# Output stores cut into 32-row pieces, a deeper put-aside window and a reordered prologue in a fused attention and two-layer MoE kernel

## The chip, the cores and the metric

The kernel runs on one core of a Trainium2 chip. The metric is the time of one execution on the device, in microseconds (us). The engines are PE (TensorE, matrix multiply; PEld is its weight load), DVE (VectorE), ACT (ScalarE), POOL (GpSimd) and SP (SyncE, which here issues transfers only). Transfers are issued from the queues of SP and ACT.

## The reference, cut to what matters

Three stages follow one another. For 8 batches of 8 heads, 576 positions and 64 columns, a softmax of `phi` over the positions condenses k and v to 32 memory rows per head, and q attends to those. The result, a matrix x of 4608 tokens by 512, goes through a gated layer (512 to 1536 and back) and then through a squared-ReLU layer (512 to 2048 and back). All is float32.

```
a = softmax(phi over s);  k_m = a^T k;  v_m = a^T v
attn = softmax(q k_m^T / 8) v_m               # -> x, 4608 x 512
xn = x / rms(x) * rms_g
x = (silu(xn @ w_gate) * (xn @ w_val)) @ w_out
out = relu(x @ w_in2)**2 @ w_out2             # 4608 x 512, written to out
```

## The kernel before, in words

Float32 products are made from float32r matmuls: each operand is split into a high and a low part (`split`: ACT rounds, line 67; the low part is a subtraction on DVE or POOL, line 71), and three matmuls stand for one.

The **prologue** computes the attention of batch 0 and prepares the first weights. The weights arrive as 64-bit values and are converted: `conv_next` starts one conversion (two ACT instructions, lines 101 and 102) and ends the one started before (two DVE instructions, lines 110 and 111, and one on POOL, line 115). The attention steps are p1 to p7 (softmax of `phi`), a2 to a7 (memory rows, transposed q), a8 and a9 (scores, lines 388 and 403), a10 to a15 (their softmax, up to the transposed `an`), a18 to a20 (output x, its squares by ACT, and their sum over the columns, line 482), a21 to a23 (reciprocal root of the mean square, from line 493, and scaling). `warm` issues idle matmuls. Instructions of an engine run in the order in which the code names them.

**Phase A** runs 8 batches in 24 slots each: matmuls for g and v (from line 803), Silu on ACT (line 849), and y, one slot later. The steps of the next batch's attention and the conversions of the remaining weights are spread over positions "a" to "d" of the slots by a plan written out by hand (`make_plan`, `slot`). y goes to memory (y1).

**Phase B** takes tokens in five pairs of column groups, the first four wide (512 columns for each half of a pair). In a pair, eight steps q make h from x by seven products in place of eight (a Strassen scheme: `h_S`, `h_A`), square it, and feed one half of the pair's columns straight into z (four PSUM banks, one for each 128 tokens); the other half of g is put aside in memory (`gd`), since the banks hold only one half. Then comes zz: a loop over f = 0 to 15 loads the put-aside tiles back (`gb`, issued on ACT's queue by `gb_load`, so many tiles ahead), splits them (`gbh`, `gbl`) and multiplies them, 12 matmuls for each f. Beside this loop the x tiles of the next pair are loaded (`x2_load`, tile `xr`) and split (`x2_step`), and the next weights are loaded (`wi2_load`: two `si` tiles and, from the second pair on, `wihb` and `wilb`).

Results leave through `out_store` (and `out_last` for the last four tiles): a PSUM bank of 128 tokens by 512 is copied to a tile `os`, and stored. The tokens lie such that 128 rows of a tile are 4 positions j of 32 rows p each, while in the output row number p * 18 + j of a batch is meant; so the destination of one store is an access pattern of 4 by 32 rows of 2 KB. A tile that crosses a batch's end takes two stores.

Of the kernel before, what the change touches and what calls it, by code (L numbers as in the profile page):

```python
# [9 lines left out]
F32 = mybir.dt.float32  # L10
# [10 lines left out]
P = 128  # L21
# [31 lines left out]
class Kernel:  # L53
# [548 lines left out]
    def make_plan(self):  # L602
        self.early, self.warm_ps = 0, None
        self.w1, self.wo, self.wph, self.wpl, self.anh, self.anl = {}, {}, {}, {}, {}, {}


        groups = [(0, hf, fs) for fs in (range(NF1 // 2), range(NF1 // 2, NF1)) for hf in range(2)]
        groups += [(b, hf, range(NF1)) for b in range(1, B) for hf in range(2)]
        self.items = [(b, hf, f, f == fs[0], f == fs[-1]) for b, hf, fs in groups for f in fs]

        def gv(ch):
            return [(kind, ch, cp) for kind in "gv" for cp in range(2)]

        def o(*fs):
            return [("o", f, 0) for f in fs]

        keys = gv(0) + gv(1) + o(0, 1) + gv(2) + o(2, 3, 4, 5) + gv(3) + gv(4) + o(6, 7) + gv(5) + o(8, 9, 10, 11)
        keys += [(c, f, 0) for f in range(NF2) for c in "iz"]
        self.raw_keys, self.conv_keys = keys, list(keys)

        self.plan = {}

        def at(n, pos, step, b, *args):
            if b < B:
                self.plan.setdefault((n, pos), []).append((step, (b, *args)))


        steps = [
            (1, "a", 0, "a7", 0),
            (1, "a", 0, "load_q", 2),  # L630
            (1, "d", 0, "t1"),
            (1, "d", 0, "a3", 0),
            (2, "a", 0, "a7", 1),
            (2, "a", 0, "load_q", 3),
            (2, "b", 0, "a2"),
            (2, "c", 0, "a3", 1),
            (2, "d", 0, "a4"),
            (0, "d", 1, "load_phi"),
            (3, "b", 0, "a5"),
            (3, "c", 0, "a6"),  # L640
            (3, "c", 0, "a7", 2),
            (3, "d", 1, "load_kv", 0),
            (4, "c", 0, "a7", 3),
            (4, "d", 1, "load_kv", 1),
            (5, "b", 0, "a8", 0),
            (5, "c", 0, "a9", 0),
            (5, "d", 1, "load_q", 0),
            (6, "b", 0, "a8", 1),
            (6, "c", 0, "a9", 1),
            (6, "d", 1, "load_q", 1),  # L650
            (7, "c", 1, "p1"),
            (8, "c", 0, "a10", 0),
            (9, "b", 1, "p3"),
            (9, "c", 0, "a10", 1),
            (11, "b", 1, "p4"),
            (11, "c", 1, "p5"),
            (12, "a", 0, "a12", 0),
            (12, "a", 0, "a12", 1),
            (12, "a", 1, "p6"),
            (13, "b", 0, "a13", 0),  # L660
            (13, "d", 0, "a13", 1),
            (14, "c", 0, "a15", 0),
            (15, "a", 0, "a15", 1),
            (15, "b", 0, "a18", 0, 0),
            (15, "c", 0, "a19", 0, 0),
            (15, "d", 0, "a18", 0, 1),
            (15, "d", 0, "a19", 0, 1),
            (16, "c", 0, "sq_add", 0),
            (16, "c", 1, "p7"),
            (17, "b", 0, "a18", 1, 0),  # L670
            (17, "c", 0, "a19", 1, 0),
            (17, "d", 0, "a18", 1, 1),
            (17, "d", 0, "a19", 1, 1),
            (18, "c", 0, "sq_add", 1),
            (19, "b", 0, "a20", 0),
            (19, "c", 0, "a21", 0, 0),
            (20, "c", 0, "a21", 0, 1),
            (21, "a", 0, "a23", 0),
            (21, "b", 0, "a20", 1),
            (21, "b", 0, "an_split", 0),  # L680
            (21, "c", 0, "a21", 1, 0),
            (22, "c", 0, "a21", 1, 1),
            (23, "c", 0, "a23", 1),
            (24, "d", 0, "an_split", 1),
        ]
        for ch in range(NCH):
            i = 14 + 2 * ch
            steps += [(i - 3, "d", 0, "wst_load", ch), (i, "a", 0, "wp_mm", ch), (i, "b", 0, "wp_ev", ch)]

        at(1, "c", "a21", 0, 1)  # L690
        at(2, "a", "a23", 0, 1)
        at(2, "d", "an_split", 0, 1)
        for b in range(B - 1):
            for i, pos, ahead, step, *args in steps:
                if (b, step) == (0, "t1"):
                    step = "t1_first"
                at(NI * b + i, pos, step, b + 1 + ahead, *args)

        for n, ch in ((1, 1), (3, 2), (7, 3), (10, 4), (13, 5)):
            at(n, "c", "wp_mm", 0, ch)  # L700
            at(n, "c", "wp_hi", 0, ch)
            at(n, "d", "wp_lo", 0, ch)
# [19 lines left out]
    def prologue(self):  # L722
# [31 lines left out]
        self.a6(0)  # L754
        self.a7(0, 2)
        self.a7(0, 3)
        self.conv_next()
        self.conv_next()
        for hf in range(2):
            self.a8(0, hf)  # L760
            self.a9(0, hf)
        self.warm(16)
        self.conv_next()
        for r in range(NR):
            self.a10(0, r, "dve")
            self.a12(0, r)
        self.conv_next()
        self.a13(0, 0, "dve")
        self.a15(0, 0)
        self.a13(0, 1, "dve")  # L770
        self.a15(0, 1)
        self.conv_next()
        self.p1(1)
        self.warm(16)
        for hf in range(2):
            for cp in range(2):
                self.a18(0, hf, cp)
                self.a19(0, hf, cp)
            if hf == 0:
                self.p3(1)  # L780
                self.p4(1)
                self.p5(1)
                self.p6(1)
        self.a20_first(0, 0)
        self.a21(0, 0, 0)
        self.wp_mm(0, 0)
        self.wp_hi(0, 0)
        self.wp_lo(0, 0)
        self.a21(0, 0, 1)
        self.a23(0, 0)  # L790
        self.an_split(0, 0, "dve")
        self.a20_first(0, 1)
        self.early = None


# [228 lines left out]
    def phase_b(self):  # L1024
# [32 lines left out]
        def gb_load(end):  # L1057
            while len(loaded) < min(end, NF2):
                i = len(loaded)
                loaded[i] = work("gb", 4, f"gb{p}_{i}", w)  # L1060
                nc.scalar.dma_start(loaded[i], gd[i])

        for _ in range(2):
# [1 line left out]
        for p in range(NPAIR):  # L1065
# [3 lines left out]
            for q in range(NQ):  # L1069
# [56 lines left out]
                piece()  # L1126
                for _ in range(2):
                    self.wo2_next(NF2)
                if q == NQ - 2 and wide:
                    self.x2_load(p + 1, 0)  # L1130
                    loaded = {}
                    gb_load(4)
            f0, f1 = NF2 - 2, NF2 - 1
            for c in range(KC):
                self.mm_z(y, self.gs[p, f0], f0, c)
# [8 lines left out]

            y = [self.ps.tile([P, T], F32, tag=f"y{c}", name=f"zz{p}_{c}") for c in range(KC)]
            for f in range(NF2 + 1):
                gb_load(f + 4)
                if f < NF2:
                    self.gs.pop((p, f), None)
                    key = ("b", p, f)  # L1150
# [4 lines left out]
                if f:  # L1155
                    self.pieces += z_pieces(2 * p + 1, y, ("b", p, f - 1), f - 1)
                    if f < NF2 - 1:
                        piece()
                        piece()
                if f == 2:  # L1160
                    self.wi2_load(p + 1, 1)
                if f < 14:
                    self.x2_step(p + 1, f // 7, f % 7)
# [3 lines left out]
    def mm_z(self, y, g, f, c):  # L1167
# [5 lines left out]
        nc.tensor.matmul(y[c], gh[:, cs], ol, start=False, stop=False)  # L1173
        nc.tensor.matmul(y[c], gl[:, cs], oh, start=False, stop=(f == NF2 - 1))  # L1174

    def out_last(self, y, t):
        nc = self.nc
        rows = self.out.rearrange("(b p j) d -> b j p d", b=B, j=J)
        b, k = divmod((NB - 1) * T + t * P, S)
        rows = rows[b, k // M : k // M + P // M]  # L1180
        if t < KC - 1:
            o = self.wb2.tile([P, DM], F32, tag="so", bufs=4, name=f"os_last{t}")
            if t % 2:
                nc.scalar.activation(o, y[t], AF.Copy)
            else:
                nc.vector.tensor_copy(o, y[t])
            nc.sync.dma_start(rows, o)
            return

        for i in range(2):  # L1190
            cs = slice(i * DM // 2, (i + 1) * DM // 2)
            o = self.wb2.tile([P, DM // 2], F32, name=f"os_end{i}")
            if i:
                nc.scalar.activation(o, y[t][:, cs], AF.Copy)
                nc.scalar.dma_start(rows[:, :, cs], o)
            else:
                nc.vector.tensor_copy(o, y[t][:, cs])
                nc.sync.dma_start(rows[:, :, cs], o)

    def out_store(self, n, y, first, end):  # L1200
        nc = self.nc
        rows = self.out.rearrange("(b p j) d -> b j p d", b=B, j=J)
        for t in range(first, end):
            o = self.wb2.tile([P, DM], F32, tag="so", bufs=4, name=f"os{n}_{t}")
            if t % 2:
                nc.vector.tensor_copy(o, y[t])
            else:
                nc.scalar.activation(o, y[t], AF.Copy)

            c0 = n * T + t * P  # L1210
            c = c0
            while c < c0 + P:
                b, k = divmod(c, S)
                e = min(c0 + P, (b + 1) * S)
                nc.sync.dma_start(rows[b, k // M : k // M + (e - c) // M], o[c - c0 : e - c0])
                c = e


# [27 lines left out]
```

## Time and profile before

| | |
|---|---|
| median of 3 runs | 1665.89 us (1664.92 to 1667.12) |
| the profiled execution's own time | 1667.58 us |
| its span, first to last instruction | 1665.7 us |
| mean granted clock of TensorE | 0.966 of full speed |
| PE busy (matmul) | 1570.0 us, 94% |
| DVE, ACT, POOL busy | 1014.2, 590.6, 391.0 us |

Times in the rows are us from the start of the span. A busy PE isn't PE at its peak, since matmuls are pipelined and their ends are modelled. The granted clock 1.00 is 2.4 GHz and 0.50 is 1.2 GHz. The DMA share is the mean busy share of the core's 16 DMA engines.

### The profile page before, as it was taken

The numbers are of one execution on the slowest core, as the hardware profiler recorded it, in microseconds if no ns is written. First come the engines' busy times: TensorE is split into PE (matmuls) and PEld (weight loads), VectorE is DVE, ScalarE is ACT, GpSimd is POOL, SyncE is SP. The second block draws the span as 40 slices with busy tenths as digits, with TensorE's granted clock in tenths as the row PEclk, the third lists the DMA queues.
The fourth block names the chain that finished last, engine by engine and source line by source line (L and its number), as shares of the span: only waits on it lengthen the run. The fifth ranks groups of instructions, "written<-read, shape, count | busy, mean of one in ns | idle before, by whom it ended". The sixth has DMA issues, their size and how long they took to land.

```text
span 1665.7 us, 26522 instructions
## 1 busy us (share of the span) xinstructions
PE 1570.0 (94%) x10298; PEld 1317.0 (79%) x10298; DVE 1014.2 (61%) x1713; ACT 590.6 (35%) x1206; POOL 391.0 (23%) x411
## 2 busy tenths in 40 slices
PE   5587999999999999999999999999899989999996
PEld 3365688888978888898998877888688868887885
DVE  4887665757466475625348875566466656664563
ACT  2456435444343544434343323211321133112321
POOL 1376534434343444424322200000000000000000
PEclk7689899999999999999999999999999999999998
DMA  9797574464747454323124465335524553435351
GB/s 265 231 274 279 196 222 174 156 187 170 206 174 203 176 176 140 121 63 141 53 97 169 168 205 162 127 131 185 158 86 149 174 175 94 161 129 185 96 169 57
DMA packets 140866, 269.92 MB, mean 162 GB/s; under 512 B 28484, under 2 KB 70724, under 8 KB 134596
## 3 DMA queue, kind: packets, MB, share of 16 engines
q1 hardware_dynamic: 127664, 248.95, 45.6%
q10 hardware_dynamic: 13076, 19.27, 4.0%
q8 instruction: 81, 1.33, 0.3%
q14 instruction: 45, 0.37, 0.1%
HBM read 208.28 MB, written 59.90 MB: 161 GB/s over the span
## 4 chain that ended last, share of the span: by engine, by line
PE 79%; DMA 7%; DVE 6%; ACT 3%; POOL 2%; issue 2%; SPq 0%; ACTq 0%; DVEq 0%; POOLq 0%
PE y L819 5%; PE y L820 5%; PE y L821 5%; PE z L1172 4%; PE z L1174 4%; PE z L1173 4%; PE h_S L1012 4%; PE h_S L1010 4%; PE h_S L1011 4%; PE v L803 3%; PE h_A L1010 3%; PE h_A L1012 3%; PE h_A L1011 3%; PE g L803 3%; DMA out_dram<-os 3%; PE wp L532 3%
## 5 line engine op out<-in xcount | busy, mean ns | idle before, releaser
L71 POOL TENSOR_TENSOR ul<-sl,uh 128x288 fp32r<-128x288 f32 x192 | 166.8, 869 | 369.4 <-ACT uh L67 368.7
L819 PE MATMUL y<-uh,woh 128*128 128x288 f32 x768 | 236.2, 308 | 0.0
L820 PE MATMUL y<-uh,wol 128*128 128x288 f32 x768 | 228.4, 297 | 0.8 <-POOL wol L71 0.8
L821 PE MATMUL y<-ul,woh 128*128 128x288 f32 x768 | 227.3, 296 | 0.0
L67 ACT ACTIVATE gh<-c 128x512 fp32r<-128x512 f32 (+1 forms) x96 | 53.8, 561 | 401.6 <-DVE c L1045 401.6
L853 DVE TENSOR_TENSOR sl<-sl,v 128x288 f32<-128x288 f32 x192 | 86.1, 448 | 178.8 <-PE v L805 139.7
L819 PEld LDWEIGHTS y<-uh,woh 128*128 128x128 f32 x768 | 145.4, 189 | 16.4 <-issue 15.7
L67 ACT ACTIVATE uh<-sl 128x288 fp32r<-128x288 f32 x192 | 85.2, 444 | 182.6 <-DVE sl L853 182.6
L820 PEld LDWEIGHTS y<-uh,wol 128*128 128x128 f32 x768 | 145.9, 190 | 1.7 <-POOL wol L71 1.0
L821 PEld LDWEIGHTS y<-ul,woh 128*128 128x128 f32 x768 | 145.7, 190 | 0.0
L849 ACT ACTIVATE sl<-g 128x288 f32<-128x288 f32 x192 | 78.6, 409 | 167.6 <-PE g L805 164.6
L803 PE MATMUL g<-anh,wph 128*128 128x288 f32 x384 | 120.1, 313 | 13.9 <-ACT sl L849 10.7
L1172 PE MATMUL z<-bzh,gh 128*128 128x512 f32 x320 | 126.0, 394 | 0.0
L1174 PE MATMUL z<-bzh,gl 128*128 128x512 f32 x320 | 125.6, 393 | 0.0
L803 PE MATMUL v<-anh,wph 128*128 128x288 f32 x384 | 120.4, 314 | 5.1 <-DVE sl L853 5.1
L1173 PE MATMUL z<-bzl,gh 128*128 128x512 f32 x320 | 125.0, 391 | 0.0
L1172 PE MATMUL zz<-bzh,gbh 128*128 128x512 f32 x256 | 103.5, 404 | 17.2 <-ACT gbh L67 17.2
L804 PE MATMUL g<-anl,wph 128*128 128x288 f32 x384 | 115.6, 301 | 0.0
L804 PE MATMUL v<-anl,wph 128*128 128x288 f32 x384 | 115.4, 301 | 0.0
L805 PE MATMUL v<-anh,wpl 128*128 128x288 f32 x384 | 114.8, 299 | 0.0
L805 PE MATMUL g<-anh,wpl 128*128 128x288 f32 x384 | 114.4, 298 | 0.0
L550 DVE TENSOR_TENSOR wpl<-wp,wph 128x512 fp32r<-128x512 f32 x96 | 61.3, 679 | 79.0 <-ACT wph L544 78.9
(221 smaller groups left out, 3728.6 us busy)
## 6 DMA issues: line engine op xcount, KB each, us to landing
w<-w SPq DMA_DIRECT2D x48, 1024.0 KB
si<-w_i SPq DMA_DIRECT2D x80, 256.0 KB
q<-in_q_dram SPq DMA_DIRECT2D x128, 144.0 KB
gd<-c SPq DMA_DIRECT2D x64, 256.0 KB
gb<-gd ACTq DMA_DIRECT2D x64, 256.0 KB
y<-ys SPq DMA_DIRECT2D x16, 576.0 KB
raw_i<-in_moe_w_in_dram SPq DMA_DIRECT2D x16, 512.0 KB
raw_z<-in_moe_w_out_dram SPq DMA_DIRECT2D x16, 512.0 KB
```

The costliest lines, as they stand in the source:

```text
L67: nc.scalar.activation(hi, src, AF.Copy)
L71: eng.tensor_tensor(lo, src, hi.bitcast(F32), op=ALU.subtract)
L803: nc.tensor.matmul(out, wh[:, r, cs], ah[:, r], start=(r == 0), stop=False)
L804: nc.tensor.matmul(out, wh[:, r, cs], al[:, r], start=False, stop=False)
L805: nc.tensor.matmul(out, wl[:, r, cs], ah[:, r], start=False, stop=(r == NR - 1))
L819: nc.tensor.matmul(y, hi[:, cs], uh, start=first, stop=False)
L820: nc.tensor.matmul(y, lo[:, cs], uh, start=False, stop=False)
L821: nc.tensor.matmul(y, hi[:, cs], ul, start=False, stop=last)
L1010: nc.tensor.matmul(out, wh[:, cs], xh, start=(kk == 0), stop=False)
L1172: nc.tensor.matmul(y[c], gh[:, cs], oh, start=(f == 0), stop=False)
L1173: nc.tensor.matmul(y[c], gh[:, cs], ol, start=False, stop=False)
L1174: nc.tensor.matmul(y[c], gl[:, cs], oh, start=False, stop=(f == NF2 - 1))
```

## The change

It has four parts, which together touch the prologue, the plan and phase B.

1. Every store of the output is cut into stores of 32 rows, one for each j (`store_rows`). Of the last four tiles, the first goes by SP's queue, the second by ACT's, the third by POOL's, and the last in two halves by SP's and ACT's.
2. Put-aside tiles are loaded into seven places in place of four: the three places of `sw`, which held weights of the last layer during the first pair, take part. The window of `gb_load` is 7 in place of 4.
3. In phase B, `x2_load` of the next pair's first half stands one step q earlier, and `wi2_load` stands in iteration 10 of the zz loop in place of 2.
4. In the prologue, batch 0's scores and their softmax stand ahead of the first weight conversions, the sum of squares of the first half stands ahead of batch 1's softmax of `phi`, whose steps p4 and p5 follow later; p6 of batch 1 (the exponentials) moves from the prologue to position "c" of slot 0.

```
+        at(0, "c", "p6", 1)
...
-        self.conv_next()
-        self.conv_next()
         for hf in range(2):
             self.a8(0, hf)
             self.a9(0, hf)
         self.warm(16)
-        self.conv_next()
         for r in range(NR):
             self.a10(0, r, "dve")
             self.a12(0, r)
         self.conv_next()
+        self.conv_next()
         self.a13(0, 0, "dve")
         self.a15(0, 0)
+        self.conv_next()
         self.a13(0, 1, "dve")
         self.a15(0, 1)
         self.conv_next()
+        self.warm(16)
+        for cp in range(2):
+            self.a18(0, 0, cp)
+            self.a19(0, 0, cp)
+        self.a20_first(0, 0)
         self.p1(1)
-        self.warm(16)
-        for hf in range(2):
-            for cp in range(2):
-                self.a18(0, hf, cp)
-                self.a19(0, hf, cp)
-            if hf == 0:
-                self.p3(1)
-                self.p4(1)
-                self.p5(1)
-                self.p6(1)
-        self.a20_first(0, 0)
+        self.conv_next()
+        self.p3(1)
+        for cp in range(2):
+            self.a18(0, 1, cp)
+            self.a19(0, 1, cp)
         self.a21(0, 0, 0)
         self.wp_mm(0, 0)
         self.wp_hi(0, 0)
+        self.p4(1)
+        self.a21(0, 0, 1)
         self.wp_lo(0, 0)
-        self.a21(0, 0, 1)
         self.a23(0, 0)
         self.an_split(0, 0, "dve")
         self.a20_first(0, 1)
+        self.p5(1)
...
-                loaded[i] = work("gb", 4, f"gb{p}_{i}", w)
+                if i % 7 < 3:
+                    loaded[i] = self.wb.tile([P, T], F32, tag="sw", bufs=3, name=f"gb{p}_{i}")
+                else:
+                    loaded[i] = work("gb", 4, f"gb{p}_{i}", w)
                 nc.scalar.dma_start(loaded[i], gd[i])
...
+                if q == NQ - 3 and wide:
+                    self.x2_load(p + 1, 0)
                 if q == NQ - 2 and wide:
-                    self.x2_load(p + 1, 0)
                     loaded = {}
-                    gb_load(4)
+                    gb_load(7)
...
-                gb_load(f + 4)
+                gb_load(f + 7)
...
-                if f == 2:
+                if f == 10:
                     self.wi2_load(p + 1, 1)
...
+    def store_rows(self, dma, b, k, o, cs=slice(0, DM)):
+        rows = self.out.rearrange("(b p j) d -> b j p d", b=B, j=J)
+        for i in range(o.shape[0] // M):
+            dma.dma_start(rows[b, k // M + i, :, cs], o[i * M : (i + 1) * M])
...
     def out_last(self, y, t):
+        if t == 1:
+            nc.scalar.activation(o, y[t], AF.Copy)
+            self.store_rows(nc.scalar, b, k, o)
+        elif t < KC - 1:
+            nc.vector.tensor_copy(o, y[t])
+            self.store_rows((nc.sync, nc.gpsimd)[t // 2], b, k, o)
+        else:
+            for i, dma in ((0, nc.sync), (1, nc.scalar)):
...
+                self.store_rows(dma, b, k, e, cs)
...
-                nc.sync.dma_start(rows[b, k // M : k // M + (e - c) // M], o[c - c0 : e - c0])
+                self.store_rows(nc.sync, b, k, o[c - c0 : e - c0])
```

## Rows read from the trace of the kernel before

**Rows 1.** The page, part 4: the chain that ended last, shares by engine.

```profile
PE 79%; DMA 7%; DVE 6%; ACT 3%; POOL 2%; issue 2%; SPq 0%; ACTq 0%; DVEq 0%; POOLq 0%
```

**Rows 2.** Windows: length, busy (xcount) of five engines, PEclk, DMA share, GB/s.

```profile
1000.00:1018.00 18.00, 14.09 (x48) 10.60 (x47) 7.32 (x13) 5.07 (x9) 0.00 (x0) 0.81 0.61 206
1030.00:1048.00 18.00, 18.00 (x81) 14.87 (x80) 9.67 (x16) 6.30 (x11) 0.00 (x0) 1.00 0.15 45
1174.00:1204.00 30.00, 25.44 (x101) 19.27 (x100) 13.37 (x21) 9.82 (x17) 0.00 (x0) 0.94 0.61 193
1347.00:1377.00 30.00, 26.32 (x105) 20.23 (x104) 14.01 (x23) 10.36 (x18) 0.00 (x0) 0.94 0.66 198
1520.00:1535.00 15.00, 11.87 (x50) 8.74 (x49) 4.75 (x11) 3.67 (x7) 0.00 (x0) 1.00 0.65 231
```

**Rows 3.** Timeline and chain around the first zz: start, length, what.

```profile
997.46 0.50 PE L1172 MATMUL zz<-bzh,gbh 128*128 128x512 f32 x1 [0.53 <-ACT gbh L67]
...
997.01 12.33 DMA out_dram<-os
...
1009.42 0.33 ACTq L1061
...
1010.53 0.80 PE zz L1172
```

**Rows 4.** Waits of SP's queue: total us, times, longest.

```profile
SPq L205 <- DMA kv<-in_v_dram: 17.3, 9, 2.9
...
SPq L1242 <- DMA out_dram<-os_end: 11.3, 1, 11.3
```

**Rows 5.** Windows at the end and while q loads are issued.

```profile
1655.00:1663.00 8.00, 0.00 (x0) 0.00 (x0) 0.00 (x0) 0.00 (x0) 0.00 (x0) 0.50 0.26 100
10.00:15.00 5.00, 3.49 (x67) 2.55 (x71) 1.98 (x6) 2.83 (x5) 0.00 (x0) 0.50 1.13 287
```

**Rows 6.** Timeline of the end: the last tile's copy and its two stores.

```profile
1651.54 0.42 DVE L1197 COPY os_end<-z 128x256 f32<-128x256 f32 x1
...
1652.22 1.08 SPq L1198 DMA_DIRECT2D out_dram<-os_end  x1
1652.41 1.14 ACTq L1195 DMA_DIRECT2D out_dram<-os_end  x1
```

**Rows 7.** One line's instructions: issue of a store and a q load, ns min/median/max.

```profile
L1215 SPq DMA_DIRECT2D out_dram<-os x36: 522/584/2536, 995.6 to 1576.4; - x36
...
L205 SPq DMA_DIRECT2D q<-in_q_dram x128: 310/419/2157, 3.5 to 711.7; - x128
```

**Rows 8.** Timeline of the prologue: start, length, what, [idle before].

```profile
3.94 1.02 DVE L226 TENSOR_REDUCE m<-ph 128x128 f32<-128x512 f32 x1 [2.96 <-DMA ph<-in_phi_dram]
...
25.72 2.13 PE L388 MATMUL sc<-qt,kt 64*32 64x288 f32 x20 [1.74 <-DVE qt L376]
...
30.04 0.43 DVE L110 TENSOR_SCALAR cv_g<-cv_g 128x512 uint32<-128x512 uint32 x1 [4.37 <-ACT cv_g L101]
...
31.11 1.57 DVE L403 STREAM_TRANSPOSE L<-sc 128x288 f32<-128x288 f32 x4
...
44.72 0.69 DVE L111 SCALAR_TENSOR_TENSOR cv_v<-raw_v,cv_v 128x512 uint32<-128x512 uint32 x1
45.33 1.92 DVE L226 TENSOR_REDUCE m<-ph 128x256 f32<-128x1024 f32 x1
...
51.53 1.36 ACT L274 ACTIVATE ph<-ph 128x1024 f32<-128x1024 f32 x2 [4.53 <-DVE ph L264]
...
55.01 0.46 DVE L493 TENSOR_SCALAR sqt<-ss 128x288 f32<-128x288 f32 x1 [3.19 <-PE ss L482]
...
61.28 0.61 PE L803 MATMUL g<-anh,wph 128*128 128x288 f32 x1 [3.22 <-ACT anh L67]
...
62.76 1.28 ACT L849 ACT_TABLE_LOAD   x1
```

**Rows 9.** Windows: the first 20 us of the main loop.

```profile
62.00:82.00 20.00, 10.28 (x120) 7.14 (x121) 19.48 (x30) 11.98 (x22) 10.92 (x10) 0.59 0.83 250
```

More of the change, by code (lines that the diff above doesn't have):

```diff
@@ L1174, in mm_z @@
         nc.tensor.matmul(y[c], gl[:, cs], oh, start=False, stop=(f == NF2 - 1))
+    def store_rows(self, dma, b, k, o, cs=slice(0, DM)):
+        rows = self.out.rearrange("(b p j) d -> b j p d", b=B, j=J)
+        for i in range(o.shape[0] // M):
+            dma.dma_start(rows[b, k // M + i, :, cs], o[i * M : (i + 1) * M])
     def out_last(self, y, t):
         nc = self.nc
-        rows = self.out.rearrange("(b p j) d -> b j p d", b=B, j=J)
         b, k = divmod((NB - 1) * T + t * P, S)
-        rows = rows[b, k // M : k // M + P // M]
         if t < KC - 1:
             o = self.wb2.tile([P, DM], F32, tag="so", bufs=4, name=f"os_last{t}")
[L1183 to L1198, printed above, removed]
+        if t == 1:
[6 more added lines that the diff above has]
+            for i, dma in ((0, nc.sync), (1, nc.scalar)):
+                cs = slice(i * DM // 2, (i + 1) * DM // 2)
+                e = self.wb2.tile([P, DM // 2], F32, name=f"os_end{i}")
+                if i:
+                    nc.scalar.activation(e, y[t][:, cs], AF.Copy)
+                else:
+                    nc.vector.tensor_copy(e, y[t][:, cs])
+                self.store_rows(dma, b, k, e, cs)
     def out_store(self, n, y, first, end):
         nc = self.nc
-        rows = self.out.rearrange("(b p j) d -> b j p d", b=B, j=J)
         for t in range(first, end):
```

## The prediction

> **What bounds the kernel now.** I read the page's chain first, then stretches. The chain lies on PE for 79% of the span and on DMA for 7% [rows 1]: phase A and phase B are mostly matmul time, and the change removes no matmul. So I looked for stretches in which PE does fewer matmuls than it could. There are three kinds: the prologue, the passage from z to zz in each of the four wide pairs, and the end.
>
> The pairs: in an undisturbed stretch 18 us hold 81 matmuls of 512 columns, 0.222 us each [rows 2]. The four stretches around z to zz hold 48 in 18 us, 101 in 30, 105 in 30 and 50 in 15; full ones would hold 81, 135, 135 and 67.5. So 33, 34, 30 and 17.5 are missing, 114.5 x 0.222 = 25.4 us. This includes the clock, which falls to 0.81 and 0.94 in the mean after PE has stood still.
>
> What PE waits for is in the chain: a store of `os` lands after 12.33 us, at 1009.34; only then does ACT issue its next load of `gb` (1009.42), make `gbh` behind it, and let zz go on (1010.53) [rows 3]. That load shares no datum with that store. But counting back in the code's order (four stores, gb4, gb5, two si, wihb, wilb, gb6), the third store is the eighth transfer before gb6. SP's q loads wait for kv loads in the same way [rows 4], which share nothing with them either. I read from both that the ninth transfer of the two queues is not issued before the first of them has landed: slow stores hold places that ACT's loads need, and ACT stands still at the load, the split behind it.
>
> Why a store is slow: at the end nothing but four tiles' stores run, at a DMA share of 0.26 and 100 GB/s [rows 5], which is 4 of 16 engines at 25 GB/s. The destination's outer dimension is 4 (the j of 128 rows). A q load has 32 rows and an outer dimension of 32, and while q loads are issued the share is 1.13 [rows 5].
>
> **The change, part by part.**
>
> *Stores of 32 rows, at the end.* Now the last four tiles, 1024 KiB, take 10.5 us at 100 GB/s: DVE's last half copy starts at 1651.54, the last issue ends at 1653.55, SP's final wait of 11.3 us [rows 4] begins behind its own issue at about 1653.3 and ends at 1664.6, and 1.1 later the span is over [rows 6]. Afterwards 16 engines move the same bytes in a quarter, 2.6 us, mostly beside the issues. The issue of a 32-row transfer takes 0.42 us (q's median), at best 0.31; that of a 128-row store 0.58 [rows 7]. ACT has the most to do. Tile 1 is ready two tiles (6 x 0.222) before 1651.54, its copy at about 1650.8; four issues reach 1652.5; the half tile's copy takes 0.42 as on DVE; then come four more issues, each behind the landing of the eighth before. A landing: the very first load of the program is used at 3.94 [rows 8], so at most 3.9 from issue to use for 256 KiB beside other loads; for 64 KiB alone I say 3. So the second four go out by 1655.2, have landed by 1658.2, and the span ends at 1659.3, 6.4 less. Tile 2 goes by POOL, of which the trace shows no transfer. Bounds: below, 0.31 each as on SP, done before ACT; above, a full 3 us one after another, 1651.6 + 12 + 1.1 = 1664.7, a gain of 1.0. I take 1 us each and 3 for the last landing, nearer to SP's rows, which hides it behind ACT. For the end: 6.4, between 1 and 9. The Trainium skill ("DMA: Bandwidth & Descriptors", "Anatomy of one DMA") gives a transfer issued by POOL about 2.0 us of fixed cost, most of it the wait for the last byte's receipt; an estimate by it alone, four wholly in turn, ends near 1661 and leaves 4.7 of the 6.4.
>
> *Stores of 32 rows, tiles put aside and moved loads, in the pairs.* `gb` is loaded seven ahead, not four (three of seven in the `sw` slots, which w2's last splits have left by then). A load issued in iteration f now feeds iteration f + 6: its own landing is 6 x 12 x 0.222 = 16 us away. The four loads of `wi2_load` go from iteration 2 to 10, behind xr and all of gb; six iterations, 16 us, remain until the next pair. `x2_load` goes one q earlier; the gd stores queued behind it on SP have four `c` buffers, a q of some 15 us, before DVE misses one. The three more gb issues at q = 6 stand on ACT ahead of the copy `p`; it may come some 4 us late, but PE has four banks, three products and pieces of 12 x 0.222 = 2.7 us, before it misses it. All these I cost at nothing.
> What stays is the wait for the eighth. zz starts at 997.46 [rows 3], the first bank is copied out 9 matmuls, 2 us, before, so sixteen stores leave SP from about 995.5 at 0.42 us, and ACT's first load in the zz loop (gb7) stands right behind them in order: it waits for somewhere between the fifth and the ninth store, issued at 997.2 to 998.9, landed by 999.5 to 1001.5. PE wants the gbh behind it one tile (2.7 us) after zz's start, at about 1000.2. So PE loses between 0 and 2 us in each pair; I take 1.2, together 4.8. The next such waits move by 0.42 while PE needs 2.7 per tile. The eviction of the banks between z and zz, about 0.7 per pair (three matmuls' places), is in the 25.4 and stays. The sum: 25.4 - 4.8 - 2.8 = 17.8, rounded to 18. Bounds: 25 (no new wait), and 8 (four stalls of 3.5 us stay).
>
> *SP's queue.* 41 store issues become 148. Per z stage SP has 16 x 0.42 = 6.7 us of stores where 4 x 0.58 stood; next on SP comes xr at iteration 6, 16 us after zz's start, which hides it. If that cover is gone it is a rival, below.
>
> *Prologue.* Now DVE's first L110 waits until 30.04 for ACT and the weights, with the four score transposes L403 queued behind it until 31.11, though the scores were ready at 25.72 + 2.13 = 27.85 [rows 8]. Afterwards the second half's two run from 27.85 and end near 28.7, not 32.7: 4.0 earlier. From there to the conversion's L111 behind the last `an` transpose (44.72) stands as much DVE work as now, 12.0 us: 40.7. From that L111 to the first a21 (55.01) it is 10.3 now: batch 1's softmax, the second half's x and its squares stand ahead of the row sums. Afterwards DVE has there the rest of L111 (0.7), p1 (1.92 and some 0.4), one more conversion end (0.43 + 0.69) and p3's reduction (some 0.4), 4.5, with `a20_first` on PE beside them: a21 near 45.5, or 46 as ACT's exps now stand ahead of the first conversion. From a21 to the first g matmul it is 61.28 - 55.01 = 6.3 as now: near 52.4, 8.9 earlier. p5, two subtractions over the tile that p1 reduces (at most its 1.92 and 0.4, I take 1.7), follows now, so DVE enters the main loop 7.2 earlier. That counts, since DVE is busy 19.48 of the next 20 us [rows 9]: the stage runs at DVE's pace.
> Against it: p6 moves behind the first Silu. It takes its 1.36 us along, and two more table loads of 1.28 (to exp and back) [rows 8]: 3.9 on ACT, ahead of a conversion for which DVE waits. ACT is idle 8 of those 20 us [rows 9], so between 0 and 3.9 reaches DVE; I take 2. Of the 5.2 left I carry 4.5, since POOL's part of the conversions and the loads may take some back. Bounds: 8, and nothing.
>
> **Sum.** 18 + 6.4 + 4.5 = 28.9. The profiled span of 1665.7 becomes 1636.8 (the run's own time, 1.9 more, 1638.7); from the median of the runs, 1665.89, it is 1637.
>
> **Rivals.**
> *A store cut in four isn't faster.* The engines would stay at 4 in effect. For it: no store of 32 rows is in this trace; against it: the share of 1.13 beside the q loads. Then the end gains nothing, gb7 waits for half of 1 MB at 100 GB/s, 5 us and more, so of the pairs' gain about 9 remain, and with 4.5 from the prologue the time is 1652. The Trainium skill speaks for this rival ("DMA: Bandwidth & Descriptors", "Rules for kernel authors"): two transfers to halves of the partitions serialize and aren't worth the cut, and small ones should be joined. By that rule the cut gives nothing; the share of 0.26 speaks against it here, as the whole store isn't spread to begin with.
> *The prologue gives nothing*: ACT is ahead of DVE by less than I think, and table loads and conversions take back what came earlier: 1665.9 - 24.4 = 1641.5.
> *The wait for the eighth costs ACT nearly as much as now*: stores under load land after 5 us, 4 x 3.5 stay: 1647.
> *Slower: SP's issues.* If a 32-row store costs x, 16 of them push xr back by 16x - 16 us in each of four pairs; from x = 1.45 on that eats the whole 28.9. At the longest q issue, 2.16 [rows 7], it is 4 x 18.5 = 74 lost, less 28.9: 1711. Against it: the median of 0.42.
>
> **Numbers.** Forecast 0.70; prologue nothing 0.14; the wait as now 0.07; not spread 0.05; slower 0.04. The likeliest gives 1637. Low end: all upper bounds, 25 + 9 + 8 = 42, 1624. High end: it takes in the first three rivals, 1652. A measurement of this kernel can tell about 0.2% (3.3 us) from no change, and all cases but the last are beyond that: faster 0.95, same 0.02 (x near 1.45), slower 0.03.
>
> **What would show it.** At the end, the span over some 8 us behind DVE's last half copy, not 14, with a DMA share well above 0.26. In the zz loop no PE wait for gbh above 2 us, none at its fourth tile, and the clock at 1.00. The first g matmul near 52, and two more table loads in the loop's first iterations. It is wrong if ACT's gb issues still wait over 3 us for stores, if POOL's four stores end last by far, or if the main loop's lead of 7 us is gone when the conversions end.

## The result

The changed kernel takes 1627.24 us (median of 4 runs, 1626.99 to 1628.49), the kernel before 1665.41 on the same chip: a ratio of 0.9772, with a 95% interval of 0.9758 to 0.9787, or 38 us less. The forecast was 1637 with a range of 1624 to 1652. The profiled execution has a span of 1626.7 us (1665.7 before).

| | before | after |
|---|---|---|
| median of the runs, us | 1665.41 | 1627.24 |
| span of the profiled execution, us | 1665.7 | 1626.7 |
| first zz (first pair), us | 997.46 | 992.07 |
| DVE's last half copy, us | 1651.54 | 1620.00 |
| from there to the span's end, us | 14.1 | 6.7 |

So of the 39.0 us between the two spans, 5.4 were there before the first zz (prologue and phase A), 26.2 came between the first zz and the last half copy (654.1 to 627.9 us), and 7.4 at the end.

The page's chain, by engine, to be set beside [rows 1]:

```profile
PE 83%; DVE 6%; ACT 3%; DMA 3%; POOL 2%; issue 2%; SPq 0%; ACTq 0%; POOLq 0%; DVEq 0%
```

DMA's share of the chain fell from 7% to 3%, and PE's rose from 79% to 83%. Stores of `os` stand in the chain of before four times, for 9.1 to 12.3 us each (the first in [rows 3]); in the changed kernel's chain they stand twice:

```profile
990.52 1.67 DMA out_dram<-os
...
1164.86 1.92 DMA out_dram<-os
```

Windows of the changed kernel, each as far behind its pair's first zz as the one of [rows 2] was, and the undisturbed stretch last (length, busy time and count of PE, PEld, DVE, ACT, POOL, then granted clock, DMA share, GB/s):

```profile
994.60:1012.60 18.00, 18.00 (x81) 14.88 (x81) 10.33 (x17) 6.51 (x11) 0.00 (x0) 1.00 0.60 170
1161.20:1191.20 30.00, 29.93 (x132) 24.28 (x131) 18.52 (x31) 12.88 (x23) 0.00 (x0) 1.00 0.60 186
1327.30:1357.30 30.00, 30.00 (x134) 24.82 (x133) 19.05 (x30) 13.18 (x24) 0.00 (x0) 1.00 0.64 188
1493.80:1508.80 15.00, 15.00 (x68) 12.42 (x67) 8.29 (x17) 5.78 (x12) 0.00 (x0) 1.00 0.66 185
1030.00:1048.00 18.00, 18.00 (x80) 14.68 (x80) 10.15 (x16) 3.89 (x8) 0.00 (x0) 1.00 0.15 44
```

PE does 81, 132, 134 and 68 matmuls where it did 48, 101, 105 and 50, at a granted clock of 1.00 throughout (0.81, 0.94, 0.94 and 1.00 before). These stretches no longer differ from the undisturbed one.

Timeline of the changed kernel around its first zz, to be set beside [rows 3] (start, length, what, idle before and its releaser):

```profile
990.13 9.76 SPq L1185 DMA_DIRECT2D out_dram<-os  x16
...
992.07 0.50 PE L1177 MATMUL zz<-bzh,gbh 128*128 128x512 f32 x1 [0.51 <-ACT gbh L67]
...
992.92 0.35 ACTq L1065 DMA_DIRECT2D gb<-gd  x1
...
993.31 0.63 ACT L67 ACTIVATE gbh<-gb 128x512 fp32r<-128x512 f32 x1 [0.78 <-DVE gbl L71]
```

ACT's load in the zz loop leaves at 992.92, in the midst of SP's sixteen stores, and the split behind it waited 0.78 us for DVE and for no store.

How long SP takes for one issue of these stores (ns, min/median/max), and what it waited for among the first sixteen (985 to 1000: total us, times, longest):

```profile
L1185 SPq DMA_DIRECT2D out_dram<-os x128: 314/419/1992, 990.1 to 1552.3; - x128
```

```profile
SPq L1185 <- DMA gb<-gd: 2.5, 2, 1.8
```

An issue takes 0.42 us in the median. The 9.76 us for sixteen hold 2.5 in which SP stood until two of ACT's `gb` loads had landed.

The end of the changed kernel: its timeline [rows 6], SP's last wait [rows 4], and a window [rows 5]:

```profile
1620.00 0.42 DVE L1206 COPY os_end<-z 128x256 f32<-128x256 f32 x1
1620.33 2.19 POOL L1185 DMA_DIRECT2D out_dram<-os_last  x4 [656.41 <-DVE os_last L1196]
1620.82 2.07 SPq L1185 DMA_DIRECT2D out_dram<-os_end  x4
1621.12 0.38 ACT L1204 ACTIVATE os_end<-z 128x256 f32<-128x256 f32 x1 [1.87 <-DVE os_end L1206]
1621.53 2.10 ACTq L1185 DMA_DIRECT2D out_dram<-os_end  x4
```

```profile
SPq L1250 <- DMA out_dram<-os_end: 2.6, 2, 2.4
```

```profile
1620.00:1626.00 6.00, 0.00 (x0) 0.00 (x0) 0.43 (x2) 0.38 (x1) 2.19 (x4) 0.70 0.58 164
```

ACT's issues end last, at 1623.63; SP then waits 2.4 us for them to land, where it waited 11.3. Share and rate (0.58, 164 GB/s) are means over a window in which the issues, not the bytes, set the pace; before they were 0.26 and 100 with nothing but bytes left to move.

The prologue of the changed kernel, to be set beside [rows 8]:

```profile
28.92 1.81 DVE L403 STREAM_TRANSPOSE L<-sc 128x288 f32<-128x288 f32 x4 [1.26 <-PE sc L388]
...
34.90 0.43 DVE L110 TENSOR_SCALAR cv_g<-cv_g 128x512 uint32<-128x512 uint32 x1 [1.30 <-ACT cv_g L101]
...
44.15 0.69 DVE L111 SCALAR_TENSOR_TENSOR cv_v<-raw_v,cv_v 128x512 uint32<-128x512 uint32 x1
...
49.63 0.42 DVE L240 TENSOR_REDUCE mc<-mt 128x2 f32<-128x256 f32 x1 [1.41 <-PE mt L239]
49.97 0.45 DVE L493 TENSOR_SCALAR sqt<-ss 128x288 f32<-128x288 f32 x1
...
56.23 0.40 PE L804 MATMUL g<-anh,wph 128*128 128x288 f32 x1 [1.99 <-ACT anh L67]
...
57.70 1.28 ACT L850 ACT_TABLE_LOAD   x1
...
62.44 1.28 ACT L274 ACT_TABLE_LOAD   x1
63.73 1.36 ACT L274 ACTIVATE ph<-ph 128x1024 f32<-128x1024 f32 x2
...
67.36 1.28 ACT L850 ACT_TABLE_LOAD   x1
```

The first g matmul comes at 56.23, 5.05 us earlier. But this execution was late before anything had been changed: its first scores came at 23.63, in the kernel before at 21.65. A second execution of the changed kernel (e12_after, below) shows what is usual:

```profile
21.56 1.18 PE L388 MATMUL sc<-qt,kt 64*32 64x288 f32 x8 [0.37 <-ACT kt L362]
...
55.02 0.54 PE L804 MATMUL g<-anh,wph 128*128 128x288 f32 x1 [1.99 <-ACT anh L67]
```

### The profile page after: what moved, and what is told of

It is laid out like the page before. It is cut to its first block, busy times and chain, and to the rows that moved or that the text cites. A ratio compares the mean times of both kernels' runs of the same rounds, so it can differ in the third digit from the quotient of the medians.

```text
span 1626.7 us, 26611 instructions
## 1 busy us (share of the span) xinstructions
PE 1556.0 (96%) x10298; PEld 1308.7 (80%) x10298; DVE 1015.5 (62%) x1713; ACT 592.6 (36%) x1208; POOL 392.8 (24%) x415
## 4 chain that ended last, share of the span: by engine, by line
PE 83%; DVE 6%; ACT 3%; DMA 3%; POOL 2%; issue 2%; SPq 0%; ACTq 0%; POOLq 0%; DVEq 0%
PE y L820 5%; PE y L821 5%; PE y L822 5%; PE z L1177 5%; PE z L1179 4%; PE z L1178 4%; PE h_S L1013 4%; PE h_S L1011 4%; PE h_S L1012 4%; PE zz L1179 3%; PE h_A L1011 3%; PE v L804 3%; PE zz L1178 3%; PE zz L1177 3%; PE h_A L1013 3%; PE h_A L1012 3%
```

## The experiments

The theory: a whole store of 128 rows runs on 4 of 16 engines and is under way for 12 us; it does harm by holding one of eight places that SP's and ACT's transfers share, and ACT, waiting for a place, keeps zz's next split behind it. The rivals: the window of four `gb` tiles is too small in any case; the stores' bytes delay the loads' bytes; cutting a transfer doesn't help as such.

All medians with the ratio to the kernel before on the same chip (its medians: 1665.6 for the first four, 1666.6 for the next four, 1663.1 for the last four):

| kernel | us | ratio, 95% interval |
|---|---|---|
| e1_stores | 1629.3 | 0.9782 (0.9766 to 0.9797) |
| e2_window | 1642.8 | 0.9865 (0.9847 to 0.9883) |
| e3_prologue | 1660.6 | 0.9973 (0.9964 to 0.9983) |
| e4_end | 1659.5 | 0.9956 (0.9940 to 0.9972) |
| e5_pool | 1653.4 | 0.9914 (0.9887 to 0.9941) |
| e6_rows64 | 1694.2 | 1.0160 (1.0136 to 1.0184) |
| e7_p6 | 1626.1 | 0.9755 (0.9734 to 0.9776) |
| e8_nowin | 1626.1 | 0.9757 (0.9732 to 0.9781) |
| e9_split | 1621.8 | 0.9741 (0.9720 to 0.9762) |
| e10_end2 | 1621.2 | 0.9740 (0.9721 to 0.9760) |
| e11_rows16 | 1631.4 | 0.9801 (0.9781 to 0.9821) |
| e12_after | 1625.6 | 0.9766 (0.9745 to 0.9787) |

### Each part alone, on the kernel before

**e1_stores**: only `store_rows` and its calls.

```
-                nc.sync.dma_start(rows[b, k // M : k // M + (e - c) // M], o[c - c0 : e - c0])
+                self.store_rows(nc.sync, b, k, o[c - c0 : e - c0])
```

> The kernel before with every output store cut into stores of 32 rows (and the last four tiles' stores shared between SP, ACT and POOL); the four-deep gb window, the places of the small loads and the old prologue stay. Theory (whole stores move on 4 of 16 DMA engines, stay under way for 12 us and hold places among the eight transfers that ACT's gb loads need): the cut alone removes the zz stalls and shortens the end, so of the 38 us gained it gives the pairs' 26 and the end's 7.5, less what the late small loads may take: 1632 to 1640. Rival A (the gb window of four is what starves zz, and the cut only helps at the end): about 1658. Rival B (the two parts share the pairs' gain, stores alone shorten the wait but gb6 still comes late): 1640 to 1652.

Measured 1629.3, and the theory's 1632 to 1640 was still too high: the cut alone gives 36 of the 38 us. From the first zz to the last half copy the profile has 628.1 us (627.9 in the changed kernel), and the end takes 6.7. Neither the deeper window nor the moved loads are needed for it.

**e2_window**: only the seven-deep window, `x2_load` and `wi2_load` at their new places; stores whole.

```
-                    gb_load(4)
+                    gb_load(7)
...
-                if f == 2:
+                if f == 10:
                     self.wi2_load(p + 1, 1)
```

> The kernel before with the gb window of seven, x2_load one q earlier and wi2_load at iteration 10 alone; whole stores, old end and old prologue stay. Theory (the stores' 12 us are the cause): gb loads issued ahead of the stores feed zz for seven tiles, 7 x 2.7 = 19 us, but the loads behind the stores still wait for their landing; if that wait of some 12 us is covered by the seven tiles, the pairs' gain is had this way too and the time is about 1640; if ACT's waiting gb issue keeps the gbh splits behind it, the stall stays and the time is 1655 to 1662. Rival (the window is the whole cause): 1640. Here the theory of places held by slow stores says 1655 to 1662, since what stands on ACT behind the waiting issue is the split that zz needs next.

Measured 1642.8, against what I had made of the theory (1655 to 1662). Timeline and a window of this kernel, whose first zz starts at 995.52:

```profile
993.59 3.23 SPq L1219 DMA_DIRECT2D out_dram<-os  x4
...
996.35 0.33 ACTq L1064 DMA_DIRECT2D gb<-gd  x1
...
998.12 0.33 ACTq L1064 DMA_DIRECT2D gb<-gd  x1
...
999.94 0.33 ACTq L1064 DMA_DIRECT2D gb<-gd  x1
```

```profile
998.00:1016.00 18.00, 18.00 (x81) 14.89 (x80) 10.34 (x17) 6.51 (x11) 0.00 (x0) 1.00 0.54 165
```

ACT's loads leave 1.8 us apart while four whole stores are issued and land: none of them waits for a store. With the window of seven and the small loads of `wi2_load` moved behind them they stand in another place of the order: the first load that needs the place of one of these stores leaves at 1005.18, 11.6 us behind that store's issue, and it doesn't wait. e2 doesn't separate the deeper window from the moved loads. Zz runs 81 matmuls in 18 us here too. From the first zz to the last half copy it is 632.5 us, 21.6 less than before and 4.6 more than in the changed kernel. Of these 4.6 the profile shows 4.2 as four stalls: 1.0, 0.7 and 1.2 some 22 us behind the zz of the first three pairs, where ACT waits for xr, and 1.2 at 1568. The end is the old one (14.2). So either part of the pairs' edit removes the stalls, and together they give no more than the stores alone.

**e3_prologue** (the prologue's diff alone, with its line in the plan) and **e4_end** (the new `out_last` alone; `out_store` as before):

```
+        at(0, "c", "p6", 1)
```

```
+            self.store_rows((nc.sync, nc.gpsimd)[t // 2], b, k, o)
```

> The kernel before with the new prologue and p6 behind the first Silu alone; stores and gb loads stay. Theory: the 5.4 us of lead that the changed kernel has at its first zz is all the prologue's, 1660. Rival A (the lead is given back in the main loop, where something else sets the pace): 1664 to 1666. Rival B (the unchanged first 20 us ran 1.5 to 2 us late in the one profile of the changed kernel, and typically don't): 1658.

> The kernel before with only the last four tiles' stores cut into 32 rows and shared between SP, ACT and POOL. Theory: the end is 6.7 us from DVE's last half copy instead of 14.2, so 7.5 less: 1658. Rival (the shorter end in the changed kernel is partly the earlier landing of other stores in the queue): 1661, half of it.

e3 gives 4.5 us (2.8 to 6.0, from its interval) and e4 7.3 (4.7 to 10.0), both as the theory had it. The interval of e4 begins just above the 4.6 of its rival; its profile settles it, with 6.1 us from the last half copy to the span's end (14.1 in before). The parts alone add up to 36.3 (e1, with the end) + 4.5 = 40.8, against 38.0 (0.0228 x 1665.4) and, measured once more as e12, 38.9 (0.0234 x 1663.1) for the whole: the same within the intervals.

### What the stores hold up

**e5_pool**: one word on the kernel before.

```
-                nc.sync.dma_start(rows[b, k // M : k // M + (e - c) // M], ...
+                nc.gpsimd.dma_start(rows[b, k // M : k // M + (e - c) // M], ...
```

> The kernel before with one word changed: the z and zz stores (whole, 128 rows, still on 4 of 16 engines) are issued by POOL instead of SP; end, gb window and prologue stay. Theory (a slow store does harm by holding one of the eight places that SP's and ACT's transfers share): POOL's transfers hold none of these, so gb6 no longer waits, the zz stalls go though each store still takes 12 us, and the time is 1640 to 1645, 20 to 26 less than the 1665.6 of before. Rival (the gb loads themselves are late because their bytes queue behind the stores' bytes on the four engines): the stalls stay, 1660 to 1666.

Measured 1653.4: a gain of 14 (10 to 19), short of 20. The stall of the theory is gone; another took its place. Windows of this kernel behind the first zz (996.72) and some 20 us later, POOL's stores, and ACT's split of the next x with SP's loads for it:

```profile
999.30:1017.30 18.00, 18.00 (x81) 14.91 (x80) 10.24 (x16) 6.52 (x11) 1.40 (x2) 1.00 0.58 155
1018.00:1028.00 10.00, 7.11 (x24) 5.07 (x23) 4.92 (x8) 4.55 (x8) 0.70 (x1) 0.83 0.58 158
```

```profile
995.11 0.88 POOL L1215 DMA_DIRECT2D out_dram<-os  x1 [26.29 <-ACT os L1208]
1002.78 0.71 POOL L1215 DMA_DIRECT2D out_dram<-os  x1 [6.80 <-issue]
1010.64 0.69 POOL L1215 DMA_DIRECT2D out_dram<-os  x1 [7.14 <-ACT gbh L67]
1018.86 0.70 POOL L1215 DMA_DIRECT2D out_dram<-os  x1 [7.53 <-issue]
```

```profile
1012.84 4.37 SPq L972 DMA_DIRECT2D xr<-y  x6
...
1020.79 0.63 ACT L67 ACTIVATE X11h<-xr 128x512 fp32r<-128x512 f32 x1 [8.19 <-DMA xr<-y]
```

While whole stores go out on POOL's queue, zz runs at full pace (81 in 18 us) with the same four-deep window and stores of the same shape: what had held gb6 was the place in SP's and ACT's order, not the window. gb6 leaves at 1001.08 here, at 1009.42 in before. (POOL's stores went out more slowly, so e5 alone doesn't exclude a part for their bytes; but in before gb6 wasn't late in landing, it wasn't issued until the store had landed [rows 3].)

The places can be read from the trace itself, since it has the semaphore that each transfer raises as it lands. SP's and ACT's transfers use eight semaphores between them, in turn; POOL's stores in e5 use eight others. In before, gb5, wilb, gb6 and gb7 have the semaphores of the four stores in their order, and each is issued some 0.08 us behind the landing of its store: 1002.14 and 1002.22, 1005.40 and 1005.47, 1009.34 and 1009.42, 1011.84 and 1011.92.

But POOL issued the four stores 7.7 us apart, each 0.3 us behind the landing of the one before (1002.47 and 1002.78, for instance; why it waits isn't shown), so that they were still moving when xr came: ACT's split stands 8.0 us behind xr's first issue (4.8 in the changed kernel: 1008.19 to 1012.96), ACT's gb loads stand behind that split, and PE does 24 matmuls in 10 us rather than 45. Those 21, 4.7 us, are what a pair lasts longer than in the changed kernel (171.3 against 166.5). That the stores' bytes make xr late is read from this, not tested apart; xr's loads of 256 KB take 7.1 us in the median from issue to landing here, 4.9 in the changed kernel.

**e6_rows64**: the changed kernel with two stores of 64 rows for each tile.

```
-        for i in range(o.shape[0] // M):
-            dma.dma_start(rows[b, k // M + i, :, cs], o[i * M : (i + 1) * M])
+        n = o.shape[0] // M
+        for i in range(0, n, 2):
+            e = min(i + 2, n)
+            dma.dma_start(rows[b, k // M + i : k // M + e, :, cs], o[i * M : e * M])
```

> The changed kernel with every store cut into two stores of 64 rows rather than four of 32. Theory (a transfer is spread over as many engines as its outermost dimension divides into, here 2, and always the same ones): the end's 1 MiB moves at about 50 GB/s in 21 us, so DVE's last half copy to the span's end is some 24 us rather than 6.7, 17 longer; the pairs, whose gb loads run seven ahead, lose between 0 and 4 us each: 1644 to 1661. Rival (smaller pieces and more of them under way are what helps): 1627 to 1632.

Measured 1694.2, slower than the kernel before and far above the range: the end was sized well, the pairs were not. A window at the end, SP's last wait, and SP's stores and ACT's waits around the first zz:

```profile
1672.00:1690.00 18.00, 0.00 (x0) 0.00 (x0) 0.00 (x0) 0.38 (x1) 1.22 (x2) 0.55 0.17 54
```

```profile
SPq L1252 <- DMA out_dram<-os_end: 18.8, 1, 18.8
```

```profile
989.36 16.10 SPq L1187 DMA_DIRECT2D out_dram<-os  x8
```

```profile
ACT gbh L67 <- DMA out_dram<-os: 8.4, 2, 6.7
ACT X11h L67 <- DMA xr<-y: 7.4, 1, 7.4
```

The 54 GB/s are about half of the 100 with which whole stores moved [rows 5], although each tile is now two transfers. They include POOL's two transfers, 15 GB/s and 0.06 of the share; SP's and ACT's packets alone have 39 GB/s and 0.11, which is 1.8 of 16 engines where the whole stores had 0.26, 4.2 engines: an outer dimension of two, two engines, and the same two for both pieces. The end takes 22.1 us from the last half copy (24 expected, with all four tiles on two engines). The Trainium skill ("DMA: Bandwidth & Descriptors", "Why a DMA increments its semaphore by 16 and not by 1") says that a transfer uses the largest number of engines up to 16 that divides both sides' outermost dimensions, on SP's and ACT's queues the lowest-numbered ones; the shares of 0.26 for an outer 4 and 0.11 for an outer 2 agree. The landings agree too: behind a first step at its issue, the semaphore of every whole store of 128 rows on SP's and ACT's queues takes four more steps, that of every store of 64 rows two; a store of 32 or 16 rows and a `gb` or q load takes sixteen.

In the first pair SP needs 16.1 us for eight issues, and the deeper window no longer covers: ACT waits for stores again (8.4). The three whole pairs last 35 us longer together than in the changed kernel, the stretch behind the last pair's zz 17, the end 15: the 67 us. So of "in four, of 32 rows" it is the 32 that counts, as the outermost dimension.

**e11_rows16**: the changed kernel with the z and zz stores in 16 rows, 32 issues for four tiles.

```
+        for r in range(0, o.shape[0], M // 2):
+            dma.dma_start(rows[b, (k + r) // M, r % M : r % M + M // 2], o[r : r + M // 2])
```

> The changed kernel with the z and zz stores cut into 16 rows, not 32 (the last four tiles stay at 32): 32 issues for four tiles where there were 16, at 0.61 us each some 19.5 us of SP. Theory (SP's issues begin 2 us before zz and the next xr is due 16 us after its start; what is late by 1 to 2 us is covered by the gb tiles put aside): the same as the changed kernel, 1625 to 1630. Rival (the prediction's slower one: all that goes beyond 16 us is lost in each of the four pairs): 3.5 x 4 = 14 more, 1641.

Measured 1631.4, 5.8 more than the changed kernel measured beside it (e12): neither. SP's queue and ACT's split of the next x:

```profile
989.05 18.76 SPq L1190 DMA_DIRECT2D out_dram<-os  x32
1007.91 3.80 SPq L973 DMA_DIRECT2D xr<-y  x6
```

```profile
1012.29 0.63 ACT L67 ACTIVATE X11h<-xr 128x512 fp32r<-128x512 f32 x1 [5.41 <-DMA xr<-y]
```

An issue still takes 0.42 us in the median, 13.4 for 32; most of the rest of the 18.76 is 3.6 us in which SP waits for the landing of `gb` loads. (The 0.61 us each of the expectation had that wait in it.) xr leaves 16.9 us behind zz's start (990.99), against 16.1 in the changed kernel: of the rival's 3.5 us a pair, 0.8 arrive at xr, because the issues begin 2 us before zz. The three whole pairs are 0.7 us longer each than in e12, and 2.9 are lost behind the last pair's zz. The rival's mechanism exists, at under half the price that was reckoned.

### The rest of the change, and a faster version

**e7_p6**: the changed kernel with `p6(1)` right behind `p5(1)` in the prologue, out of the main loop's plan. **e8_nowin**: the changed kernel without the put-aside tiles and moved loads.

```
-        at(0, "c", "p6", 1)
...
         self.p5(1)
+        self.p6(1)
```

```
-                gb_load(f + 7)
+                gb_load(f + 4)
```

> The changed kernel with batch 1's exp (p6) kept in the prologue, right behind p5, so that the two extra table loads and the exp don't stand between the first Silus. Theory (p6 behind the first Silu costs the 3.6 us of lead that are lost between the first and the second Silu): 1 to 3.5 less than the changed kernel, 1624 to 1626. Rival (ACT has slack there and DVE's pace takes the gain back): 1627.

> The changed kernel without the put-aside tiles and moved loads: a gb window of four again, x2_load and wi2_load at their old places; stores of 32 rows and the new prologue stay. Theory (with short stores the window has nothing left to hide): the same as the changed kernel within 2 us, 1625 to 1629. Rival (the window still covers something, such as late loads behind sixteen stores): 1631 or more.

Both measure 1626.1, and with ratios of 0.9755 and 0.9757 neither can be told from the changed kernel (0.9772 and 0.9766). In e7's profile the second Silu comes 1.4 us earlier than in e8's (65.69 against 67.06), but the third 0.2 later (81.45 against 81.25): p6 and its table loads make the way from the first Silu to the second 9.7 us (6.0 in before), and by the third nothing of it is left. The window of seven does nothing once the stores are short.

**e9_split**: e8_nowin, with the first gb tile of a pair split before the z banks are copied out. **e10_end2**: e9_split with the last tile cut by rows between DVE and ACT, four stores rather than eight.

```
+            gb_split(0)
             for c in range(KC):
                 self.mm_z(y, self.gs[p, f1], f1, c)
                 self.out_store(2 * p, y, c, c + 1)
```

```
-                cs = slice(i * DM // 2, (i + 1) * DM // 2)
+                rs = slice(i * P // 2, (i + 1) * P // 2)
```

> The changed kernel with a gb window of four again (as e8_nowin) and the first gb tile of each pair split on ACT and DVE ahead of the copies of the four z banks, not behind them. Theory (in every kernel so far PE loses 0.7 and 0.3 us at the start of zz because gbh and gbl stand behind ACT's and DVE's copies of z, not because a bank isn't free): 4 x 0.98 = 3.9 less than e8_nowin, 1622. Rival (PE has to wait for the banks' copies anyway, or the copies come later by what the split takes): 1626.

> e9_split with the last tile cut between DVE and ACT by rows (64 each, all 512 columns) instead of by columns, so that it leaves in four stores of 32 rows, not eight. Theory (at the end ACT's issues are last: its last four took 2.10 us): two issues fewer on SP and ACT, less 0.25 us for the longer copies, so DVE's last copy to the span's end shortens from 6.7 to about 5.8 us: 0.9 less than e9_split, 1621. Rival (POOL's four stores land last): no change.

> The changed kernel itself once more, to stand beside the others on the same chip: 1627 (1625 to 1629).

e9 measures 1621.8, 3.9 less than the changed kernel beside it (1625.6; in the profiles it is 623.5 us from the first zz to the last half copy against 627.5), and it is the fastest of these kernels with e10 (1621.2), which can't be told from it by its time. PE and ACT of e9 around the first zz:

```profile
989.63 0.39 PE L1179 MATMUL z<-bzh,gl 128*128 128x512 f32 x1
989.86 0.39 PE L1177 MATMUL zz<-bzh,gbh 128*128 128x512 f32 x1
```

```profile
985.59 0.62 ACT L67 ACTIVATE gbh<-gb 128x512 fp32r<-128x512 f32 x1
988.01 0.60 ACT L1216 ACTIVATE os<-z 128x512 f32<-128x512 f32 x1 [1.81 <-PE z L1179]
```

Zz follows z at 0.23 us, without the 0.7 and 0.3 us that are lost there with the old order (zz at 992.07 in the changed kernel waits 0.51 for gbh): these were no eviction but two splits queued behind the copies. With the matmuls behind them it is 1.2 us a pair: in the changed kernel the four starts behind the last z (991.16) are at 992.07, 992.40, 992.94 and 993.28, 2.12 us for four steps of 0.23. e10's end takes 5.8 us in its profile (1612.99 to 1618.8), as expected, 0.9 less than e9's.

## Why the prediction was right, and where its sizes were off

The mechanism held: e5 and the semaphores show the place in the order, e1 and e6 the engines. The time came out 10 us below the forecast, inside the range, and the terms miss in both directions.

**Pairs: 18 forecast, 26.2 measured.** Two terms that were taken off are wrong. The first is the new wait for the eighth, 1.2 us in each pair, 4.8 together. It was worked out from the code's order (gb7 "stands right behind them in order"); the trace has gb7 leaving in the midst of the sixteen stores, with only DVE to wait for. The order in which SP and ACT take their places isn't the order in the code: by the semaphores gb7 comes behind the first four of the sixteen stores. The second is the 2.8 for the eviction of the banks, which by the prediction "is in the 25.4 and stays". It stays, as an order of splits and copies (e9) and no eviction, but it isn't in the 25.4: it lies at zz's start (997.46 in the first pair), and the windows of [rows 2] begin 2.0 us and more behind that, the first at 1000.00. So it was taken off a sum that didn't hold it.

In these windows the changed kernel does 111 matmuls more than before, 111 x 0.222 = 24.6 us of the 25.4. The other 1.6 of the 26.2 lie outside them, most of it one stall of 1.2 us in the last pair of before, where 1.43 us pass between the start of a matmul at 1591.85 and that of the next:

```profile
1593.28 0.36 PE L1010 MATMUL h_A<-X11h,wiha 128*128 128x256 f32 x1 [1.03 <-DVE c L1101]
```

**Which part gives it.** The prediction costed stores, put-aside tiles and moved loads as one edit. They are two ways to the same gain: stores alone 26.0 us of the pairs, window and moved loads alone 21.6, all together 26.2.

**End: 6.4 forecast, 7.4 measured.** ACT's issues are last, and they end 3.63 us behind DVE's last copy, where 3.66 had been worked out. The mis-sized term is what follows: 3 us for the last landing and 1.1 to the span's end; it took 3.1 in all, with SP waiting 2.4 of them. POOL's stores left 0.55 us apart and weren't last. The estimate by the Trainium skill's page ("DMA: Bandwidth & Descriptors", "Anatomy of one DMA"), four of POOL's transfers wholly in turn and 4.7 of gain, doesn't fit: they weren't in turn.

**Prologue: 4.5 forecast, 4.5 measured alone (e3), by two errors that cancel, which is luck.** The first g matmul came 6 us earlier (60.8 to 62.0 in the five profiles with the old prologue; 54.1 to 55.2 in eight with the new one, beside the late 56.23), not 8.9. The score transposes ended where reckoned. Then DVE stood 1.3 us for ACT, whose exps now precede the first conversion (0.5 was allowed), and 1.2 to 2.0 for PE's transpose of p1's maxima, L239, behind the row sums; that wait had not been counted. On the other side p6 with its table loads was charged 2, and by the third Silu next to nothing of it was left (e7). At the first zz the profiles with the new prologue are still 6.1 us ahead in the mean (990.0 of nine, 996.1 of five); why the times of e3 give no more than 4.5 stays open.

**SP's queue: 0.42 us an issue forecast, and 0.42 measured.** But sixteen take 9.76 us, not 6.7, because the wait for a place goes both ways: SP stands 2.5 us for two of ACT's loads, which the prediction hadn't counted. The cover held all the same: xr left 16.1 us behind zz's start.

**The rivals.** "A store cut in four isn't faster" falls with e1; the rule that two transfers to halves of the partitions aren't worth the cut (the Trainium skill, "DMA: Bandwidth & Descriptors", "Rules for kernel authors") doesn't decide here: its reason is that both halves run on all 16 engines, and neither the whole store nor e6's halves do (four landing steps and two). Where the cut makes the outermost dimension 32 it is worth 36 us (e1). "The prologue gives nothing" falls with e3, whose interval begins at a gain of 2.8 us; "the wait for the eighth costs as now" with the windows above. "SP's issues" exists, at under half its price (e11).

## What to carry to other kernels

In these runs a transfer's outermost dimension decided how many engines moved it: look for a DMA share that is a small fraction of 16 engines (0.26 here, 0.17 with halves of 64 rows) while nothing else moves, or a landing in few steps, and cut there, down to pieces that fill the engines and no further. A slow transfer can hold up another queue that waits for its place, with no datum shared. The semaphores that the transfers raise show who shares a place with whom; putting the slow one on a queue of its own shows in one run whether that place is what costs. When two edits aim at one stall, time each alone, since here either was nearly enough.

## What the hardware showed beyond that

- POOL issued whole 128-row stores 7.7 us apart (e5), each only behind the landing of the one before, but 32-row ones 0.55 us apart (2.19 for four), each some 2 us before the landing of the one before.
- A 32-row store of 64 KB landed 2.3 us after its issue in the median, a 16-row one of 32 KB after 1.8: half the bytes saved 0.5 us.
